# Attention over a long cache with a gated mix: projections in column blocks before the last sums, and the output written as four rows

## The chip, the cores and the metric

The kernel runs on one core of one Trainium2 chip. The metric is device time in microseconds (us). A run has a time and a span: the span, from the first to the last instruction on the core, is what the profile shows, and it lies about 1.8 us under the time. Every run told here was classed fast. Before the change the kernel takes 2521.2 us, so 0.1% is 2.5 us.

## The reference

One token `x` (512 numbers) attends to a cache of 65,536 keys and values for each of 32 heads; a small gated network takes the same token; a sigmoid gate mixes the two.

```
q = (x @ wq) as 32 heads of 128
p = softmax(q . k_cache / sqrt(128))            # 32 heads, 65536 keys each
a = (p . v_cache, the heads side by side) @ wo  # 4096 -> 512
b = (silu(x @ w_gate) * (x @ w_up)) @ w_down    # 512 -> 1792 -> 512
g = sigmoid(sum(x * gate_w))
return g * a + (1 - g) * b                      # 512 numbers in bf16, 1 KB
```

Keys and values are 1.07 GB and each is used once.

## The kernel before

Each head's cache comes in two chunks of 32,768 keys, so there are 64 chunks of keys and 64 of values. Three buffers of 8 MB take turns. For each chunk VectorE (DVE) multiplies the keys by the query ("products"), TensorE (PE) adds the 128 products of each key up to 8 partial sums with 16 matmuls against the identity ("sums"), DVE adds these 8 up ("gather"), ScalarE (ACT) takes exponentials, and PE multiplies by the values into `O_ps`. The loads of keys and values are issued by SyncE.

Only the end matters here. The last chunk (head 31, second half) is taken in four blocks of 64 keys a partition. Around it stand the projections of everything already known: `b_ps` (the gated network) and `a_ps` (heads 0 to 30).

```python
    def rows(key, w_v, names, cols, cname, ks):      # a projection to 512 outputs, 4 columns of 128
        group(key, [(m_x[:, b : b + 1],
                     [(w_v[:, k, bass.ds(b, P, OT)], cols[:, k : k + 1]) for k in ks])   # every 4th column
                    for b in range(OT)], names + [cname], ["m_x"])
    ...
    # last but one chunk, n == N - 2, after its fourth block:
                norm(0, H - 1)       # tot_ps: PE sums the row totals of heads 0..30; DVE inverts them
                outputs()            # oT = o_all * tot
    ...
    turn_outputs(1)
    rows("b_ps", wd, units(ws, 0, WO), hT, "hT", range(FT))              # 56 matmuls of one column
    diagonal()
    for i, j in enumerate(range(0, KPP, EK)):                            # four blocks
        block(n, j, EK)                                                  # products (DVE), sums (PE)
        if i == 0:
            dve("rest", ...)                                             # rest = (1 - g) * b
            rows("a_ps", wo, units(ws, WO, WL), M, "M", range(H))        # 128 matmuls of one column
        if i == 2:
            dve("rest2", ...)                                            # rest += g * a
        while len(todo) > 1:
            gather()
    gather()
    for m in V_END:                                                      # values in 5 pieces
        mms(("c", at), m_c[:, 0:1], [(v[:, j, :], P_sb[n % 2][:, j : j + 1]) ...])  # 256 one-column matmuls
        ...
    dve("o_last", ...)                                                   # m_c * tot
    rows("l_ps", wo_last, units(ws, WL, WL + D), o_last, "o_last", [0])  # 4 matmuls
    dve("out_sb", ...)                                                   # g * l + rest, 128 x 4
    dma("out", out[0, 0].rearrange("(p b) -> p b", b=OT), out_sb, ["out"], ["out_sb"])
```

The softmax here doesn't subtract the row's maximum and nothing guards it: scores larger than these inputs give would overflow.

## Time and profile before

| | before |
|---|---|
| time, median of the first 3 runs | 2521.22 us (2519.79 to 2521.41) |
| span of the profiled run | 2519.9 us |
| data queue's share of 16 DMA engines | 99.7% |
| PE busy, DVE busy | 79%, 50% |
| last values landed, last matmul into `m_c` done, end of span | 2511.9, 2514.7, 2519.9 us |

From the page, part 2 (busy tenths of the DMA engines in 40 slices) and part 3 (queue: packets, MB, share of 16 engines):

```profile
DMA  9999999999999999999999999999999999999998
q1 hardware_dynamic: 20880, 1087.78, 99.7%
```

The DMA engines are full from end to end. A change that moves no bytes can gain only in the last slice.

The timeline there: start, duration (both us), engine, source line, operation, output<-inputs, shapes, count, and in brackets the idle time before it and what ended it. `S_ps` are the sums; `m_x<-hT` is b_ps, `m_x<-M` is a_ps.

```profile
2466.23 15.46 PE L251 MATMUL O_ps<-slot_65,P_sb_83 128*4 128x512 bf16 x64 [1.35 <-ACT P_sb_83 L288]
...
2481.82 2.03 PE L279 MATMUL m_x<-hT,slot_66 128*128 128x1 bf16 x56
...
2484.98 3.40 PE L269 MATMUL S_ps_101<-slot_67,ident 128*128 128x512 bf16 x15
...
2488.22 4.38 PE L279 MATMUL m_x<-M,slot_66 128*128 128x1 bf16 x128
...
2492.68 5.08 PE L269 MATMUL S_ps_102<-slot_67,ident 128*128 128x512 bf16 x15
...
2498.41 4.42 DVE L338 TENSOR_TENSOR slot_67<-slot_67,q_bc_79 128x8192 bf16<-128x8192 bf16 x1
...
2506.35 3.35 PE L251 MATMUL m_c<-P_sb_84,slot_65 128*128 128x1 bf16 x128
...
2512.66 2.01 PE L251 MATMUL m_c<-P_sb_84,slot_65 128*128 128x1 bf16 x70 [1.22 <-issue]
2514.71 0.22 DVE L588 TENSOR_SCALAR o_last<-m_c,tot 128x1 bf16<-128x1 f32 x1 [4.38 <-PE m_c L251]
...
2515.38 0.22 DVE L593 SCALAR_TENSOR_TENSOR out_sb<-m_x,gval,rest 128x4 bf16<-128x4 f32 x1 [0.45 <-PE m_x L279]
2515.62 0.35 SPq L179 DMA_DIRECT2D out_dram<-out_sb  x1
```

The 256 matmuls into `m_c` take 8.3 us and contain a hole of 1.22 us ("issue": nothing that the profile shows was awaited). The semaphores in the trace say that the last values had landed at 2511.90, 0.76 us before the hole ended. From the issue of the output DMA to the end of the span it is 4.3 us, though the output is 1 KB.

From the view of a stretch of time, for 2482.89 to 2493.13 us (columns: us, busy time and count of PE, PE's weight loads, DVE, ACT, POOL, then the granted PE clock, 1.00 for whole and 0.50 for half, DMA share, GB/s); and from the DMA view (KB, and us from issue to landing):

```profile
2482.89:2493.13 10.24, 10.24 (x185) 6.36 (x165) 9.24 (x4) 0.35 (x2) 0.00 (x0) 1.00 1.04 445
```

```profile
out_dram<-out_sb SPq DMA_DIRECT2D x1, 1.0 KB, 3.0
```

### The profile page before, as it was taken

To read this page: it belongs to the slowest core of one execution; us is meant where nothing else is said; L and a number is where in the kernel's file an instruction comes from. 1 tells how busy PE (TensorE), PEld (TensorE's weight loads), DVE (VectorE), ACT (ScalarE), POOL (GpSimd) and SP (SyncE) were. 2 spreads that over 40 slices of the span, in tenths; PEclk is the share of its full clock that TensorE was granted. 3 is DMA by queue.
4 is the path that set the end of the run, shared out by engine and by line. 5 is a ranking of instruction groups with operands and counts; after the bars stand their busy time and mean duration, and the time that the engine had idled before them with its cause. 6 is when DMAs were issued, how large, how long until landed. Compare 5 with 4: busy or idle time off the path is not lost.

```text
span 2519.9 us, 15461 instructions
## 1 busy us (share of the span) xinstructions
PE 1980.9 (79%) x9115; PEld 410.4 (16%) x5153; DVE 1268.7 (50%) x290; ACT 97.9 (4%) x402; POOL 1.9 (0%) x9
## 2 busy tenths in 40 slices
PE   4787877877878778778787787787787877877888
PEld 1111111111111111111111111111111111111113
DVE  3455455464554554644645536446455455464454
ACT  0000000000000000000000000000000000000000
POOL 0000000000000000000000000000000000000000
PEclk8888988989889889899899899898988988989998
DMA  9999999999999999999999999999999999999998
GB/s 423 431 432 433 434 435 435 433 435 437 433 434 433 434 433 435 436 436 433 434 435 435 433 434 433 434 434 437 434 436 433 434 437 433 434 433 433 433 431 361
DMA packets 20903, 1088.04 MB, mean 432 GB/s; under 512 B 2450, under 2 KB 2580, under 8 KB 2836
## 3 DMA queue, kind: packets, MB, share of 16 engines
q1 hardware_dynamic: 20880, 1087.78, 99.7%
q8 instruction: 13, 0.21, 0.0%
q14 instruction: 6, 0.05, 0.0%
q10 hardware_dynamic: 4, 0.00, 0.0%
HBM read 1087.77 MB, written 0.00 MB: 432 GB/s over the span
## 4 chain that ended last, share of the span: by engine, by line
DMA 44%; PE 41%; DVE 13%; ACT 1%; issue 0%; another core or an unknown queue 0%; SPq 0%; DVEq 0%; ACTq 0%
PE O_ps L251 18%; DMA slot_67<-in_A_k_cache_dram 16%; DMA slot_65<-in_A_k_cache_dram 14%; DMA slot_66<-in_A_k_cache_dram 14%; PE S_ps_101 L269 11%; PE S_ps_102 L269 9%; DVE slot_67 L338 4%; DVE slot_66 L338 4%; DVE slot_65 L338 3%; DVE S_sb_82 L363 2%; PE m_c L251 1%; PE S_ps_101 L279 1%; PE m_x L279 1%; ACT P_sb_83 L288 1%; DMA slot_65<-in_A_wq_dram 0%; PE S_ps_102 L279 0%
## 5 line engine op out<-in xcount | busy, mean ns | idle before, releaser
L338 DVE TENSOR_TENSOR slot_67<-slot_67,q_bc_79 128x16384 bf16<-128x16384 bf16 (+1 forms) x28 | 208.2, 7469 | 143.8 <-DMA slot_67<-in_A_k_cache_dram 143.8
L363 DVE TENSOR_REDUCE S_sb_82<-S_ps_102 128x128 f32<-128x1024 f32 (+1 forms) x67 | 78.8, 1177 | 392.8 <-PE S_ps_102 L269 392.8
L338 DVE TENSOR_TENSOR slot_65<-slot_65,q_bc_78 128x16384 bf16<-128x16384 bf16 x22 | 190.2, 8689 | 146.9 <-DMA slot_65<-in_A_k_cache_dram 146.9
L338 DVE TENSOR_TENSOR slot_66<-slot_66,q_bc_78 128x16384 bf16<-128x16384 bf16 (+1 forms) x24 | 190.6, 7978 | 136.7 <-DMA slot_66<-in_A_k_cache_dram 121.2
L338 DVE TENSOR_TENSOR slot_66<-slot_66,q_bc_79 128x16384 bf16<-128x16384 bf16 x20 | 172.9, 8689 | 119.9 <-DMA slot_66<-in_A_k_cache_dram 119.9
L338 DVE TENSOR_TENSOR slot_65<-slot_65,q_bc_79 128x16384 bf16<-128x16384 bf16 x20 | 172.9, 8689 | 119.1 <-DMA slot_65<-in_A_k_cache_dram 119.1
L338 DVE TENSOR_TENSOR slot_67<-slot_67,q_bc_78 128x16384 bf16<-128x16384 bf16 x20 | 172.9, 8689 | 117.3 <-DMA slot_67<-in_A_k_cache_dram 117.3
L269 PE MATMUL S_ps_101<-slot_67,ident 128*128 128x512 bf16 x680 | 191.3, 450 | 0.0
L269 PE MATMUL S_ps_101<-slot_65,ident 128*128 128x512 bf16 x651 | 187.1, 458 | 0.0
L269 PE MATMUL S_ps_101<-slot_66,ident 128*128 128x512 bf16 x650 | 185.3, 455 | 0.0
L251 PE MATMUL O_ps<-slot_67,P_sb_83 128*4 128x512 bf16 x704 | 155.9, 383 | 27.9 <-ACT P_sb_83 L288 18.3
L251 PE MATMUL O_ps<-slot_65,P_sb_83 128*4 128x512 bf16 x704 | 155.2, 381 | 19.6 <-ACT P_sb_83 L288 19.6
L251 PE MATMUL O_ps<-slot_66,P_sb_84 128*4 128x512 bf16 x704 | 153.7, 379 | 19.3 <-ACT P_sb_84 L288 19.3
L251 PE MATMUL O_ps<-slot_65,P_sb_84 128*4 128x512 bf16 x640 | 139.7, 379 | 18.3 <-ACT P_sb_84 L288 18.3
L251 PE MATMUL O_ps<-slot_67,P_sb_84 128*4 128x512 bf16 x640 | 139.7, 379 | 18.3 <-ACT P_sb_84 L288 18.3
L251 PE MATMUL O_ps<-slot_66,P_sb_83 128*4 128x512 bf16 x640 | 139.7, 379 | 17.5 <-ACT P_sb_83 L288 17.5
L269 PE MATMUL S_ps_102<-slot_67,ident 128*128 128x512 bf16 x680 | 152.4, 382 | 0.0
L269 PE MATMUL S_ps_102<-slot_65,ident 128*128 128x512 bf16 x651 | 143.9, 379 | 0.0
L269 PE MATMUL S_ps_102<-slot_66,ident 128*128 128x512 bf16 x650 | 143.9, 379 | 0.0
L279 PE MATMUL S_ps_101<-slot_65,ident 128*128 128x512 bf16 x21 | 12.8, 608 | 134.5 <-DVE slot_65 L338 134.5
L279 PE MATMUL S_ps_101<-slot_66,ident 128*128 128x512 bf16 x22 | 13.1, 597 | 130.5 <-DVE slot_66 L338 130.5
L279 PE MATMUL S_ps_101<-slot_67,ident 128*128 128x512 bf16 x24 | 13.9, 580 | 125.4 <-DVE slot_67 L338 125.4
(89 smaller groups left out, 702.8 us busy)
## 6 DMA issues: line engine op xcount, KB each, us to landing
slot_66<-in_A_k_cache_dram SPq DMA_DIRECT2D x4, 2048.0 KB, 24.5
slot_67<-in_A_k_cache_dram SPq DMA_DIRECT2D x4, 2048.0 KB, 29.0
slot_65<-in_A_wq_dram SPq DMA_DIRECT2D x1, 4096.0 KB, 12.3
slot_66<-in_A_wo_dram SPq DMA_DIRECT2D x1, 4096.0 KB, 32.5
slot_65<-in_A_v_cache_dram SPq DMA_DIRECT2D x1, 4096.0 KB, 20.5
slot_65<-in_A_v_cache_dram SPq DMA_DIRECT2D x1, 2048.0 KB, 24.9
slot_65<-in_B_w_gate_dram SPq DMA_DIRECT2D x1, 1792.0 KB, 34.7
slot_65<-in_B_w_up_dram SPq DMA_DIRECT2D x1, 1792.0 KB, 38.4
```

The costliest lines, as they stand in the source:

```text
L251: ins = nc.tensor.matmul(out_ap, lhsT=a, rhs=b, start=start and i == 0, stop=stop and i == len(pairs) - 1,)
L269: ins = nc.tensor.add_instruction(mybir.InstMatmult(name=nc.get_next_instruction_name(), engine=mybir.EngineType.PE, ins=[nc.tensor.lower_ ...
L279: ins = nc.tensor.matmul(out_ap, lhsT=a, rhs=b, start=first, stop=last)
L288: "ACT", key, lambda: nc.scalar.activation(out=out_ap, in_=in_ap, func=func, **kw),
L338: "products", lambda: nc.vector.tensor_tensor(out=w, in0=w, in1=q_rep, op=ALU.mult),
L363: lambda: nc.vector.tensor_reduce(out=S_sb[b][:, :m], in_=S_ps[r][:, :m, :], axis=AXIS.X, op=ALU.add),
```

## The change

Intent: read the projection weights in contiguous blocks of 128 columns; do both projections before the last chunk's sums, so that they no longer stand between sums; take the row totals off the path of the last but one chunk; and write the output as 4 rows of 256 B instead of 128 pieces of 8 B. For the last, what is known of the output (`rest`, 128 x 4) is turned into 4 rows by one float32 matmul with an identity, and the last head's column is spread over `Z`, so that four matmuls give its part as 4 rows too.

```diff
-                    m_x[:, b : b + 1],
-                    [(w_v[:, k, bass.ds(b, P, OT)], cols[:, k : k + 1]) for k in ks],
+                    bank[:, b : b + 1],
+                    [(w_v[:, k, P * b : P * (b + 1)], cols[:, k : k + 1]) for k in ks],
 ...
+            if n == N - 2 and j == 2 * m:
+                sum_ps(0, H - 1)                       # PE's part of norm, two blocks earlier
             block(n, j, m)
 ...
-            elif n == N - 2 and j + m == KPP:
-                norm(0, H - 1)
-                outputs()
 ...                                                    # norm and outputs now after the last gather
-            turn_outputs(0)                            # now after O_ps
 ...
+    turn_outputs(0)
     turn_outputs(1)
-    rows("b_ps", ..., range(FT))
+    rows("b_ps", ..., range(FT), m_x, "m_x")
+    rows("a_ps", ..., range(H), m_sp, "m_sp")
     diagonal()
     for i, j in enumerate(range(0, KPP, EK)):
-        block(n, j, EK)
-        if i == 0:   (rest, a_ps)     if i == 2:   (rest2)
+        if i == 1:   (rest, rest2)
+        if i == 2:
+            mms("rest_ps", m_sp[:OT, :P], [(rest, ident_f)], ["rest", "ident_f"], ["m_sp"])
+            act("rest4", rest4, m_sp[:OT, :P], ACT.Copy, ["m_sp"], ["rest4"])
+        block(n, j, EK)
 ...
-    dve("o_last", ...)      rows("l_ps", ...)      out_sb 128 x 4
-    dma("out", out[0, 0].rearrange("(p b) -> p b", b=OT), ...)
+    dve("Z", lambda: nc.vector.tensor_scalar_mul(
+            Z[:, :: OT + 1], m_c[:, 0:1].to_broadcast([P, OT]), tot[:, h:H]), ...)
+    mms("l_ps", m_x[:OT, :P],
+        [(Z[:, OT * q : OT * (q + 1)], wo_last[:, 0, P * q : P * (q + 1)]) for q in range(OT)], ...)
+    dve("out_sb", ...)                                 # 4 x 128, with rest4
+    dma("out", out[0, 0].rearrange("(i p) -> i p", p=P), ...)
```

(Cut: tiles, memsets and selects at the start, wait lists.)

More of the change, by code (lines that the diff above doesn't have):

```diff
@@ L148 @@
     rest = sb("rest", [P, OT], f32)
+    rest4 = sb("rest4", [OT, P], f32)
+    ident_f = sb("ident_f", [P, P], f32)
+    Z = sb("Z", [P, OT * OT], bf16)
     o_row = sb("o_row", [H, Dh], bf16)
     M = sb("M", [P, H], bf16)
-    o_last = sb("o_last", [P, 1], bf16)
-    out_sb = sb("out_sb", [P, OT], bf16)
+    out_sb = sb("out_sb", [OT, P], bf16)
     S_ps = [psum.tile([P, HK, R], f32, name=f"S_ps{i}") for i in range(2)]
@@ L226 @@
     op("DVE", "oT0", lambda: nc.vector.memset(oT, 0.0), writes=["oT"])
+    op("DVE", "Z0", lambda: nc.vector.memset(Z, 0.0), writes=["Z"])
     op("DVE", "rowsum0", lambda: nc.vector.memset(rowsum, 0.0), writes=["rowsum"])
@@ L239 @@
     select("ident", ident, ones_b, "ones_b", [[-1, P]], 1)
+    select("ident_f", ident_f, ones, "ones", [[-1, P]], 1)
     select("pick", pick, ones[0:VB, 0:VB], "ones", [[-1, VB]], 1)
@@ L456, in gate, with rows @@
         )
-    def rows(key, w_v, names, cols, cname, ks):
+    def rows(key, w_v, names, cols, cname, ks, bank, bname):
         group(
@@ L468, in rows, with sum_ps @@
             ],
-            names + [cname], ["m_x"],
+            names + [cname], [bname],
         )
-    def norm(h0, h1):
+    def sum_ps(h0, h1):
         w = CH * RS
@@ L475, in norm @@
             ["ones", "rowsum"] + [("rowsum", i) for i in range(h0 * w, h1 * w)], ["m_x"])
+    def norm(h0, h1):
+        w = CH * RS
         dve(
@@ L539 @@
         if n == N - 2:
-            turn_outputs(0)
+            norm(0, H - 1)
+            outputs()
         pv(n)
@@ L553 @@
     load("v", n, V_END)
+    turn_outputs(0)
     turn_outputs(1)
-    rows("b_ps", wd, units(ws, 0, WO), hT, "hT", range(FT))
+    rows("b_ps", wd, units(ws, 0, WO), hT, "hT", range(FT), m_x, "m_x")
+    rows("a_ps", wo, units(ws, WO, WL), M, "M", range(H), m_sp, "m_sp")
     diagonal()
     for i, j in enumerate(range(0, KPP, EK)):
-        block(n, j, EK)
-        if i == 0:
+        if i == 1:
             dve("rest", lambda: nc.vector.tensor_scalar_mul(rest, m_x[:, :OT], ngval),
                 ["m_x", "ngval"], ["rest"])
-            rows("a_ps", wo, units(ws, WO, WL), M, "M", range(H))
-        if i == 2:
             dve(
@@ L566 @@
                 lambda: nc.vector.scalar_tensor_tensor(
-                    out=rest, in0=m_x[:, :OT], scalar=gval, in1=rest, op0=ALU.mult, op1=ALU.add
+                    out=rest, in0=m_sp[:, :OT], scalar=gval, in1=rest, op0=ALU.mult, op1=ALU.add
                 ),
-                ["m_x", "gval", "rest"], ["rest"],
+                ["m_sp", "gval", "rest"], ["rest"],
             )
+        if i == 2:
+            mms("rest_ps", m_sp[:OT, :P], [(rest, ident_f)], ["rest", "ident_f"], ["m_sp"])
+            act("rest4", rest4, m_sp[:OT, :P], ACT.Copy, ["m_sp"], ["rest4"])
+        block(n, j, EK)
         while len(todo) > 1:
@@ L585 @@
         if at == 0:
+            sum_ps(h, H)
             norm(h, H)
         at += m
-    dve("o_last", lambda: nc.vector.tensor_scalar_mul(o_last, m_c[:, 0:1], tot[:, h:H]),
-        ["m_c", ("tot", h)], ["o_last"])
-    rows("l_ps", wo_last, units(ws, WL, WL + D), o_last, "o_last", [0])
+    dve(
+        "Z",
+        lambda: nc.vector.tensor_scalar_mul(
+            Z[:, :: OT + 1], m_c[:, 0:1].to_broadcast([P, OT]), tot[:, h:H]
+        ),
+        ["m_c", ("tot", h)], ["Z"],
+    )
+    mms(
+        "l_ps", m_x[:OT, :P],
+        [(Z[:, OT * q : OT * (q + 1)], wo_last[:, 0, P * q : P * (q + 1)]) for q in range(OT)],
+        ["Z"] + units(ws, WL, WL + D), ["m_x"],
+    )
     dve(
@@ L593 @@
         lambda: nc.vector.scalar_tensor_tensor(
-            out=out_sb, in0=m_x[:, :OT], scalar=gval, in1=rest, op0=ALU.mult, op1=ALU.add
+            out=out_sb, in0=m_x[:OT, :P], scalar=gval[:OT, :], in1=rest4,
+            op0=ALU.mult, op1=ALU.add,
         ),
-        ["m_x", "gval", "rest"], ["out_sb"],
+        ["m_x", "gval", "rest4"], ["out_sb"],
     )
-    dma("out", out[0, 0].rearrange("(p b) -> p b", b=OT), out_sb, ["out"], ["out_sb"])
+    dma("out", out[0, 0].rearrange("(i p) -> i p", p=P), out_sb, ["out"], ["out_sb"])
     op("SP", "end", None, reads=["out"])
```

## The prediction

> **What bounds it.** The page gives the data queue 99.7% of sixteen DMA engines' span: 1,087.8 MB at 432 GB/s. The change leaves those bytes and the first 2,440 us alone; only the end can move. By the DMA view the last values land by about 2511.9 us; the span ends at 2519.9: at most 8 us (0.3%) are open.
>
> **The end before (timeline).** The last score sums end at 2506.4; 256 one-column matmuls into m_c run to 2514.68, at 26 ns each, with a hole of 1.22 us at 2511.44 put down to "issue". A 16 KB packet of the instruction queue starts at 2510.31 (DMA view), so I read the hole as instruction supply. [...] Then o_last 0.22, four matmuls 0.27, out_sb 0.22, the output DMA issued at 2515.62, 3.0 us to landing (DMA view), 1.3 us to the end.
>
> **What changes.**
> 1. Row totals of heads 0 to 30 are summed two blocks earlier. DVE's last two gathers of the last but one chunk no longer wait for them (2464.5 before; about 2459.4 and 2463.1 after), so its O_ps starts 2 us earlier (2466.2 before) and the last value loads are issued 2 us earlier. Worth nothing for landing: the queue is full of keys until 2492.
> 2. Projections use contiguous 128-column weights instead of every fourth column: 56 took 2.03 us and 128 took 4.38 (35 ns each), contiguous m_c ones 26 ns. Estimate: 1.5 and 3.4 us.
> 3. a_ps now stands before the last sums, and the second products wait for rest2, hence a_ps. Estimate: a_ps ends 2486.2 to 2487.3 (an instruction hole of up to 1 us may fall in it), second products start near 2487.4 instead of 2484.0. Before, a_ps sat between the sums and delayed the fourth products to 2498.4. Adding 4.42 + 0.69 us a block, these now begin 2497.0 to 2497.6, and m_c 0.3 to 1.6 us before 2506.35.
> 4. Turning rest into rows (a float32 matmul, about 0.4 us, and a copy, 0.25) hides behind products.
> 5. After m_c: Z costs what o_last did. Four 128-column matmuls at half clock: 0.3 to 0.6 us instead of 0.27; out_sb about 0.34 instead of 0.22. Together +0.3.
> 6. The output goes as 4 runs of 256 B instead of 128 of 8 B. [...] First and last completions lie 1.7 us apart before; I expect landing in 1.6 to 2.0 us, 1.0 to 1.4 less.
>
> The added memset and select at the start run while the first weights are awaited (13.4 us): free.
>
> **Sum.** m_c 0.7 earlier, tail +0.3, output DMA -1.2: -1.6 us, 0.06%. Predicted 2519.6 us, range 2516.5 to 2522.5. Chances: faster by over 2% 0.005, within 2% 0.99, slower 0.005.
>
> **What would show it.** Span about 2518.3; data queue still 99.7%; O_ps of the last but one chunk at 2464.2; a_ps at 26 ns each, before all of the last chunk's sums; fourth products near 2497.3; the m_c hole still there; output landing under 2.1 us.
>
> **What would make it wrong.** The clock halves for stretches of 3.4 us (about 2493.2 to 2496.6 before, windows view): elsewhere, it moves the sums by up to 1.7 us. A hole in a_ps may eat step 3's gain. Few descriptors may be slower than hoped. Runs before differ by 1.6 us, as much as the effect.

0.7 us earlier, 0.3 later and 1.2 less make -1.6 us, and 2519.6 us. The times of the work that is new (float32 matmul, copy, four 128-column matmuls, out_sb, landing) are estimates; after the change they measured 0.38, 0.27, 0.59, 0.34 and 1.17 us.

## The result, and the profile after

| | before | after |
|---|---|---|
| time, median of 4 runs | 2521.18 us | 2520.10 us (2518.92 to 2520.33) |
| span of the profiled run | 2519.9 | 2518.5 |
| start of b_ps | 2481.8 | 2479.2 |
| start of m_c | 2506.35 | 2507.52 |
| end of m_c | 2514.67 | 2514.75 |
| end of m_c to issue of the output DMA | 0.96 | 1.31 |
| issue of the output DMA to end of span | 4.26 | 2.47 |

The ratio of fast runs is 0.9996, with a 95% interval of 0.9979 to 1.0013. A ratio is the mean time of one kernel's fast runs over that of the other's of the same rounds, so not quite the ratio of the medians. That interval is some 4 us either way; what is argued below about single microseconds rests on the traces, and on runs side by side on one chip, where the scatter can be seen.

The same lines after the change. The page:

```profile
DMA  9999999999999999999999999999999999999998
q1 hardware_dynamic: 20744, 1087.78, 99.7%
```

The timeline (a_ps now writes `m_sp`):

```profile
2464.15 13.97 PE L255 MATMUL O_ps<-slot_65,P_sb_83 128*4 128x512 bf16 x64 [1.17 <-ACT P_sb_83 L292]
...
2479.23 1.55 PE L283 MATMUL m_x<-hT,slot_66 128*128 128x1 bf16 x56
...
2480.65 2.75 PE L283 MATMUL m_sp<-M,slot_66 128*128 128x1 bf16 x103
...
2485.19 0.82 PE L283 MATMUL m_sp<-M,slot_66 128*128 128x1 bf16 x25 [1.79 <-issue]
...
2486.19 4.42 DVE L342 TENSOR_TENSOR slot_67<-slot_67,q_bc_79 128x8192 bf16<-128x8192 bf16 x1
...
2488.14 5.87 PE L273 MATMUL S_ps_103<-slot_67,ident 128*128 128x512 bf16 x15
...
2494.05 0.69 DVE L367 TENSOR_REDUCE S_sb_81<-S_ps_103 128x64 f32<-128x512 f32 x1 [3.44 <-PE S_ps_103 L273]
...
2499.59 4.42 DVE L342 TENSOR_TENSOR slot_67<-slot_67,q_bc_79 128x8192 bf16<-128x8192 bf16 x1
...
2507.52 3.38 PE L255 MATMUL m_c<-P_sb_84,slot_65 128*128 128x1 bf16 x128
...
2511.20 3.55 PE L255 MATMUL m_c<-P_sb_84,slot_65 128*128 128x1 bf16 x128
...
2514.79 0.23 DVE L603 TENSOR_SCALAR Z<-m_c,tot 128x4 bf16<-128x4 f32 x1 [3.04 <-PE m_c L255]
...
2515.70 0.34 DVE L615 SCALAR_TENSOR_TENSOR out_sb<-m_x,gval,rest_97 4x128 bf16<-4x128 f32 x1 [0.68 <-PE m_x L255]
2516.06 0.34 SPq L181 DMA_DIRECT2D out_dram<-out_sb  x1
```

The stretch 2482.89 to 2493.13, and what SyncE waited for at the end (us in total, times, longest):

```profile
2482.89:2493.13 10.24, 8.45 (x66) 3.04 (x50) 4.55 (x2) 0.00 (x0) 0.00 (x0) 0.50 1.02 435
```

```profile
SPq L181 <- DMA out_dram<-out_sb: 0.8, 1, 0.8
```

What is to be seen: the last but one chunk's `O_ps` starts 2.1 us sooner and the projections are cheaper (27 ns instead of 35 for each matmul of a_ps). `O_ps` also takes 1.49 us less, which the change cannot be credited with: in the profile of before the clock was half for 3.41 us of it (2465.87 to 2469.28), and in none of the other 13, two of them of the old order. So of the 2.6 us by which b_ps starts sooner, 1.49 are the clock's; against them, the turning of the outputs now stands between `O_ps` and b_ps and takes 1.1 us. But a_ps has a hole of 1.79 us that was not there, the first sums run at half clock (5.87 us for 15 matmuls, where 3.40 is the full-clock figure), and the gather that waits for them comes at 2494.05. Nothing of the head start is left at the start of m_c; it comes 1.17 us later than before. The hole in m_c is gone instead, so m_c ends where it did. Then the tail is 0.36 us longer, and the output DMA lands 0.8 us after its issue is over, or 1.17 us after the issue began (by the trace's semaphores, 2516.06 to 2517.23), instead of 3.0. 0.08 + 0.36 - 1.79 us is the 1.4 us between the two spans.

### The profile page after: what moved, and what is told of

It reads as the page before. It is cut to its first block, busy times and chain, and to the rows that moved or that the text cites. A ratio compares the mean times of both kernels' runs of the same rounds, so it can differ in the third digit from the quotient of the medians.

```text
span 2518.5 us, 15470 instructions
## 1 busy us (share of the span) xinstructions
PE 1979.8 (79%) x9117; PEld 409.9 (16%) x5155; DVE 1268.7 (50%) x291; ACT 98.2 (4%) x403; POOL 2.2 (0%) x10
## 4 chain that ended last, share of the span: by engine, by line
DMA 44%; PE 41%; DVE 13%; ACT 1%; issue 0%; another core or an unknown queue 0%; SPq 0%; DVEq 0%; ACTq 0%
PE O_ps L255 18%; DMA slot_67<-in_A_k_cache_dram 16%; DMA slot_65<-in_A_k_cache_dram 14%; DMA slot_66<-in_A_k_cache_dram 14%; PE S_ps_103 L273 11%; PE S_ps_104 L273 9%; DVE slot_67 L342 4%; DVE slot_66 L342 4%; DVE slot_65 L342 3%; DVE S_sb_82 L367 2%; PE m_c L255 2%; PE S_ps_103 L283 1%; ACT P_sb_83 L292 1%; DMA slot_65<-in_A_wq_dram 0%; PE m_x L283 0%
```

## The experiments

Theory: the whole gain is the output DMA; the new order earns nothing, because with a_ps ahead of the sums PE meets a hole that is a wait for instructions and the clock halves, and because the end of m_c is pinned by other things (such a hole, the last values). Rivals: the order earns part of the gain; the holes are waits for data; the clock halves by its own rhythm; the second products' wait for rest2 sets the pace, as the prediction had it.

### The new output alone, and the new order alone

`e1_old_order` is the kernel before with the new output and contiguous weights, everything else in the old order; `e2_old_output` is the changed kernel with the old output.

```diff
  e1, on the kernel before:
+        if i == 3:  (rest_ps, rest4)     + Z, l_ps, out_sb 4 x 128, output as (i p) -> i p; contiguous rows()
  e2, on the changed kernel:
-    Z, l_ps, out_sb 4 x 128, rest_ps, rest4
+    o_last, l_ps, out_sb 128 x 4, output as (p b) -> p b; rows() with every 4th column
```

> The kernel before with the new output alone (four rows, Z, rows of rest turned by the float32 matmul, contiguous weights), the order of sums, totals and projections left as before. Theory A (the whole gain is the output DMA; the new order is worth nothing): output issue to end of the span about 2.5 us as in the changed kernel, against 4.3 before; m_c ends between 2513.0 and 2514.7; span 2517.0 to 2518.6. Theory B (the new order earned part of the gain): m_c ends at 2514.7 as before and the span is 2518.5 or more, and the old-output run with the new order shows a gain too.

> The changed kernel with the old output (128 rows of 4, strided weights, o_last), its order kept. Theory A (gain is the output DMA): output issue to end of span 4.3 us again, 1.8 us more than in the changed kernel; span 2519.5 to 2521, no better than before. Theory B: span under 2519.3.

Measured, both on one chip with before at 2522.0 us (median of 7):

| | time, median of 4 | span (profiled) | m_c start, end | output issue to end of span |
|---|---|---|---|---|
| e1: new output, old order | 2519.06 | 2518.4 | 2505.82, 2514.60 | 2.48 |
| e2: old output, new order | 2521.25 | 2519.6 | 2506.37, 2514.56 | 4.10 |

The gain goes with the output; the new order by itself is within the scatter (0.75 us under before, whose own runs differ by 2.6). Two things stay open here. The four rows need the contiguous weights, so e1 has both, and what the cheaper weight reads earn was not tested alone. And the tail explains 1.4 us; the medians of e1 and before differ by 2.9. e2 was expected at a span of 2519.5 to 2521, and its profiled run is there (the others: 2518.9 to 2519.6). In e1, m_c began 1.7 us sooner than in the changed kernel and still ended only 0.15 us sooner: there was a hole of 1.72 us in it.

### What the holes are

`e3_shift32` and `e4_shift95` add harmless one-column matmuls, each two instructions (the timeline of before lists 128 weight loads and 128 matmuls for a_ps), while PE is idle before the last but one chunk. They change no data and no waits near the end; they only move all later instructions in PE's program.

```diff
         m = EK if n in (0, N - 2) else HK
+        if n == N - 2:
+            mms("shift", m_x[:, 0:1], [(ones_b, ident[:, 0:1])] * 32, ...)     # e4: * 95
```

> The changed kernel with 32 one-column matmuls (64 instructions, weight load and matmul each) added in PE's idle time before the last but one chunk. Instruction supply: the hole in a_ps moves from after 103 matmuls to after 71 (a tolerance of 3), and a hole of 0.3 to 1.2 us may come back in the second part of m_c near its 25th matmul. Rival, a wait for data (weights wo, M) or the clock: the hole stays after 103 matmuls or at the same time, about 2483.4.

> The same with 95 one-column matmuls (190 instructions). Instruction supply: the hole in a_ps is gone, since its place is then about 8 matmuls into a_ps[...]; a_ps is 3.4 us in one piece and ends near 2484.1; a hole of about 1 us shows in the first part of m_c near its 92nd matmul. For the clock: if it drops near 2482.9 without any hole, the one-column matmuls and not the hole make it drop; if it does not drop, the hole did. Span within 1.5 us of the changed kernel.

The timeline of e3 (cut to a stretch):

```profile
2479.53 1.98 PE L283 MATMUL m_sp<-M,slot 128*128 128x1 bf16 x71
2484.03 1.68 PE L283 MATMUL m_sp<-M,slot 128*128 128x1 bf16 x57 [2.52 <-issue]
...
2511.94 2.91 PE L255 MATMUL m_c<-P_sb,slot 128*128 128x1 bf16 x104 [1.66 <-issue]
```

The hole moved from after 103 matmuls to after 71: by 32, exactly the number put in. A hole returned in m_c after 24 matmuls of its second part (25 expected; it took 1.66 us, where 0.3 to 1.2 were expected). Data cannot explain that; the weights wo had landed at 2472.8 in the changed kernel, and the place moved with the program, not with the time. So I read the holes as PE waiting for its own instructions. The queue that the profile names "instruction" has a packet before each: the page of the changed kernel counts 13 packets of q8, 0.21 MB, each of 16 KB in the trace (what such a packet brings is called a page in the recorded texts). One starts at 2482.77, where the DMA view shows, for 2482.7 to 2482.9 us:

```profile
q8 instruction: 1, 0.02, 27.5%
```

Matmuls resume 2.42 us later. Over all 20 holes in a_ps and m_c, in the profiles of the twelve experiments and of the two first kernels, from that packet to the resumption it took 2.19 to 2.45 us, wherever the hole was. From the end of a hole in a_ps, beside a full data queue (98.1% from 2480 to 2486 in the changed kernel), to the next packet it took 3.5 to 4.1 us (7 cases), from the end of one in m_c, with few values or none left to load, 1.1 to 1.6 us (13 cases). Whether the full queue makes this difference was not tested, and what sets a packet off the trace does not show. In the changed kernel's m_c the packet came at 2510.10, when the values were nearly all in; PE reached the place about 2512.8, 2.7 us after the packet, and there was no hole.

In e4 the hole in a_ps is gone, and a shorter one, which ends 2.24 us after the next packet, stands before the first sums:

```profile
2479.76 3.42 PE L283 MATMUL m_sp<-M,slot 128*128 128x1 bf16 x128
...
2485.38 0.61 PE L283 MATMUL S_ps<-slot,ident 128*128 128x512 bf16 x1 [0.41 <-issue]
```

The hole of m_c was not after 92 matmuls of the first part, as I expected, but after 89 of the second (1.33 us): there was a packet at 2488.96, long before PE reached the first place (15 us before m_c began). A miss in detail. e3 took 2519.85 us and e4 2518.90 (medians of 4, the chip of e1 and e2); in e4's profile the span is 2517.0 and m_c starts at 2504.17. The added matmuls leave the result correct.

### The clock

In e4 the granted clock was half from 2481.93 to 2488.75 though no hole had come before it, so here no hole made it fall. The stretch up to its 0.41 us hole, in the windows view (the clock is the third figure from the right):

```profile
2481.93:2484.97 3.04, 3.04 (x55) 2.93 (x52) 2.43 (x4) 0.00 (x0) 0.00 (x0) 0.50 1.00 420
```

`e8_wide` sets one 512-column matmul, its result thrown away, ahead of every 8 one-column matmuls of the projections.

```diff
+                if i % 8 == 0:
+                    nc.tensor.matmul(S_ps[1][:, :64, :], lhsT=ident, rhs=wo[:, 0, :], start=True, stop=True)
                 ins = nc.tensor.matmul(o, lhsT=a, rhs=c, start=first, stop=last)
```

> The changed kernel with one 512-column matmul (result thrown away) ahead of every 8 one-column matmuls of the two projections: 23 of them, about 5 us more of PE work before the first sums. If a stretch of one-column matmuls is what lets the clock halve: no half clock between 2478 and the end of the first sums, and the first sums take 3.8 us instead of 5.2 to 6.4. If the clock halves for another reason (its own rhythm, the DMA load, the wide matmuls before): half clock in 2480 to 2492 as in all five runs so far, and first sums of 5 us or more. Span within 2 us of the changed kernel.

Windows view of e8, for the projections and for the first sums (the granted clock is the third figure from the right):

```profile
2478.00:2488.60 10.60, 10.60 (x219) 7.81 (x215) 5.10 (x4) 0.20 (x1) 0.00 (x0) 1.00 1.02 433
2488.60:2492.40 3.80, 3.70 (x18) 0.15 (x2) 3.80 (x2) 0.00 (x0) 0.00 (x0) 1.00 1.09 466
```

The clock stayed whole and the first sums took 3.6 us, against 6.3 in the changed kernel. In the trace of before, the half-clock stretches that end before m_c last 3.41 us (8), 6.83 (46), 10.24 (10) and, once, 20.48. In the new order b_ps, a_ps and the one-column matmuls of the diagonal after them last 6.6 us (e4, no hole in them) to 9.7 us (e2); in all 9 profiles with that order and without the wide matmuls the clock halved 1.5 to 3.7 us after b_ps began, and the first sums met half clock. In all 14 profiles it also halved within 2.4 to 5.3 us of the start of m_c, the other long run of one-column matmuls. PE's busy time did not tell the two clocks apart: it was 3.04 of 3.04 us in e4's stretch at half clock and 10.60 of 10.60 in e8's at whole. In the old order sums met half clock in before and e1, and none did in `f_old_order` (below); why is not shown. The wide matmuls cost about 4.7 us themselves (from the start of b_ps to the end of a_ps 9.5 us, against 4.8 in e4), so e8 gains nothing: m_c began at 2505.81. Its time had two values, 2520.0 and 2523.8, twice each. The profile, the only one of e8, is of the faster kind. The slower kind stays unexplained; its mean granted clock is lower (0.904 and 0.905 against 0.907 and 0.908), so whether the clock stayed whole there too is not known.

### The wait for rest2

> The changed kernel with rest, rest2 and the turn to rows moved from the second block of the last chunk to the fourth, so that the second products no longer wait for a_ps. My prediction's step (the second products' wait for rest2 sets the pace): second products start near 2482.9 instead of 2486.2, the fourth products 2 to 3 us sooner, m_c starts near 2504.5 to 2505.5 and the span falls by 1 us or more. Rival (the first sums, which stand behind a_ps on PE and run at half clock, set the pace): second products start near 2482.9, but the first gather still waits for the first sums until 2492.4 to 2494.1, and m_c starts between 2505.9 and 2507.6, span 2518 to 2519, as in the changed kernel.

```diff
-        if i == 1:   (rest, rest2)     -        if i == 2:   (rest_ps, rest4)
+        if i == 3:   (rest, rest2, rest_ps, rest4)
```

Timeline of e5 (the second products, the first gather and what it waited for):

```profile
2483.08 4.42 DVE L342 TENSOR_TENSOR slot<-slot,q_bc 128x8192 bf16<-128x8192 bf16 x1 [0.97 <-DMA slot<-in_A_k_cache_dram]
...
2491.45 0.69 DVE L367 TENSOR_REDUCE S_sb<-S_ps 128x64 f32<-128x512 f32 x1 [3.94 <-PE S_ps L273]
```

The second products started 3.1 us sooner and the time was not used: DVE then waited 3.94 us for the first sums, which came sooner (2491.45) than the rival's 2492.4 to 2494.1. m_c started at 2505.31, 2.2 us sooner than in the changed kernel, which lies in the range that the prediction's step would have given; but b_ps itself began 2.2 us sooner in this run (2477.03). From b_ps to m_c it was 28.3 us in both (some 0.4 us of e5's are the moved operations, which now stand before its fourth products). The scatter in b_ps's start (2476.8 to 2479.2 in the profiles of the new order) goes with the clock in the chunk before: no half-clock stretch there between 2440 and 2450 us, 2476.8 to 2477.2; one of 3.4 us, 2478.0 to 2478.3; one of 6.8 us, as in the changed kernel's first profile, 2479.2. So from here on I compare b_ps to m_c. The rival stands: the first sums, behind a_ps on PE, set the pace. The time was 2519.69 us.

### The output DMA

`e7_16x64` and `e7_64x16` send other data of the same 1 KB in other shapes. Their outputs are wrong, which doesn't matter for the times.

```diff
+    out_w = sb("out_w", [16, 32], bf16)        # or [64, 8]
+    dve("out_w", ...)                          # fills it, after out_sb: the issue comes 0.26 us later
-    dma("out", out[0, 0].rearrange("(i p) -> i p", p=P), out_sb, ["out"], ["out_sb"])
+    dma("out", out[0, 0].rearrange("(i p) -> i p", p=32), out_w, ["out"], ["out_w"])
```

> The changed kernel with the output DMA sending 16 rows of 64 B of other data instead of 4 of 256 B; wrong result on purpose, to read the time from issue to the last completion (1.2 us for 4 of 256 B, 2.8 to 3.0 us for 128 of 8 B). If the many completions of 16 engines are slow: 2.4 us or more. If the tiny pieces[...] are slow: 1.1 to 1.6 us.

> The same with 64 rows of 16 B, wrong on purpose. If the pieces' size or number sets it: between the 16 x 64 B and the 128 x 8 B case, 1.6 to 2.4 us. If only the 16 completions do: the same as 16 x 64 B.

DMA views of the two, 16 rows of 64 B and then 64 rows of 16 B (last figure: us from issue to landing):

```profile
out_dram<-out_w SPq DMA_DIRECT2D x1, 1.0 KB, 1.3
```

```profile
out_dram<-out_w SPq DMA_DIRECT2D x1, 1.0 KB, 1.7
```

So 4 x 256 B, 16 x 64 B, 64 x 16 B and 128 x 8 B land in 1.17, 1.3, 1.7 and 2.8 to 3.0 us. Sixteen completions are not slow: those of 16 x 64 B and of 64 x 16 B come within 0.17 us of one another, those of 128 x 8 B (before) within 1.72 us. Size or number does it, with the largest step between 16 and 8 B. Why 8 B is so much worse stays open; I could not part the size from the number, as the output is 1 KB. Both kernels took 2520.2 us (medians of 2).

### Side by side, five rounds

Four kernels on one chip: the changed one again (`f_after`), e1 again (`f_old_order`), e4 again (`f_shift95`), and `e6_a_between`, the changed kernel with a_ps put back between the sums, and `rest` and its turn behind it.

```diff
  e6, on the changed kernel:
-    rows("a_ps", ...)                          # before the loop over blocks
         block(n, j, EK)
+        if i == 0:
+            rows("a_ps", ...)
     (rest, rest2, rest_ps, rest4 at i == 3)
```

> The changed kernel once more, beside the others of this call on one chip. Span 2517 to 2519; hole in a_ps after 103 matmuls; in m_c a hole after 56 or 57 matmuls unless the m_c matmuls start after about 2507.3 (the page comes about 2.35 us after its fetch shows in the DMA view). A second profile also tells how much of the last chunk's start is its own scatter (O_ps end 2475.5 to 2478.2 so far).

> The kernel before with the new output alone, again. If the new order is worth nothing: within 0.7 us of the changed kernel, either way.

> The changed kernel with 95 one-column matmuls ahead, again: no hole in a_ps; m_c starts near 2504 and ends near 2513.2, with the last values landed by 2512.0 to 2512.6. Faster than the changed kernel by 0.7 to 1.8 us and faster than before by 2 to 3.5 us if instruction supply is what held the changed kernel; no difference from the changed kernel if the first result was scatter.

> The changed kernel with a_ps put back after the first sums of the last chunk and rest2 and the turn to rows after it (row totals early, contiguous weights and four-row output kept). If placing a_ps ahead cost time: from the start of b_ps to the start of m_c 27.2 us or less instead of 28.0 to 28.4. Either way the end of m_c is set by the instruction page and the last values (2513 to 2514.5), so the span is within 0.8 us of the changed kernel.

| 5 runs each | time, median (range) | b_ps to m_c, us | m_c start, end | ratio to before |
|---|---|---|---|---|
| before (9 runs) | 2521.05 (2520.37 to 2521.87) | 24.5 (first profile) | 2506.35, 2514.67 (first profile) | 1 |
| f_after | 2518.76 (2518.56 to 2520.06) | 27.4 | 2504.20, 2513.02 | 0.9993 |
| f_old_order | 2518.46 (2518.11 to 2518.79) | 23.1 | 2502.34, 2512.84 | 0.9989 |
| f_shift95 | 2519.01 (2518.14 to 2519.18) | 27.3 | 2505.29, 2513.57 | 0.9990 |
| e6_a_between | 2519.71 (2518.40 to 2520.11) | 27.4 | 2505.49, 2514.22 | 0.9992 |

No fast run of the four with the new output was as slow as the fastest of before. (Even f_old_order's interval, 0.9976 to 1.0003, holds 1.) By medians they gain 1.3 to 2.6 us, of which the tail explains 1.4; as before was not profiled in this round, what lies beyond is not assigned. Among the four, the ranges overlap, and the order of kernels is not settled. f_after had its holes where they were expected, after 103 matmuls of a_ps and 56 of the second part of m_c; its span, 2516.8, was 0.2 us under the expected range. f_shift95 was expected 0.7 to 1.8 us under f_after and was not (medians 0.25 us above): a miss. Its a_ps had no hole, but its half-clock stretch was 10.24 us long this time (6.8 in e4), and m_c started 1.1 us later than in e4; f_after for its part had no half-clock stretch in the chunk before and started m_c 3.3 us sooner than the changed kernel's first profile. e6 was expected at 27.2 us or less from b_ps to m_c and had 27.4, with half clock on its first sums, and its median was 0.95 us over f_after's, not within 0.8: a miss as well. The distance is not a fair measure for e6, though: the first products cannot start before their keys land (2477.6 to 2478.0 in all profiles), and without a_ps in front PE waited 1.84 us for them, after b_ps and the diagonal.

f_old_order shows why little more is to be had from the order. Its profile has no half clock between 2446.7 and 2504.8, and m_c started 5.2 us sooner than in the changed kernel's first profile; then it waited for the values. Its timeline:

```profile
2509.81 1.01 PE L256 MATMUL m_c<-P_sb,slot 128*128 128x1 bf16 x32 [0.49 <-DMA slot<-in_A_v_cache_dram]
2511.03 0.59 PE L256 MATMUL m_c<-P_sb,slot 128*128 128x1 bf16 x16 [0.21 <-DMA slot<-in_A_v_cache_dram]
2512.26 0.58 PE L256 MATMUL m_c<-P_sb,slot 128*128 128x1 bf16 x16 [0.64 <-DMA slot<-in_A_v_cache_dram]
2512.88 0.23 DVE L598 TENSOR_SCALAR Z<-m_c,tot 128x4 bf16<-128x4 f32 x1 [6.30 <-PE m_c L256]
```

The last values landed at 2512.21, as in every kernel within half a microsecond (2511.9 to 2512.5), and m_c ended 0.6 us later. An earlier m_c cannot end sooner with these loads, as its last piece of values comes then; the changed kernel's first profile is 1.9 us above this end of m_c, its second 0.2.

The version to keep is thus the old order with the new output: the lowest median of the four, fewer edits, and the tightest range. It is 2.6 us (0.1%) under before, by medians; over the changed kernel its 0.3 us is not settled.

## Why the prediction was right or wrong

The total was right: 2519.6 us predicted, 2520.1 measured, and "within 2%" with near certainty. Luck had a part in it: by the traces m_c gave 0.8 us less than said and the output DMA 0.6 us more, and these errors nearly cancel. The stated range, 2516.5 to 2522.5, held the time of before as well, so a change without any effect would have fitted it. Three terms made the total up.

1. "output DMA -1.2" was right in kind and too small: it measured -1.79, 1.17 us to landing where I gave 1.6 to 2.0. I took what is left with few pieces as larger than it is.
2. "tail +0.3" measured +0.36: Z 0.23, four matmuls 0.59, out_sb 0.34, as costed.
3. "m_c 0.7 earlier" is the step that failed. By its end m_c was 0.08 us later, by its start 1.17 later. Inside it:
   - Row totals earlier: right. `O_ps` was said to start at 2464.2 and started at 2464.15; landing times did not move.
   - Contiguous weights at 26 ns: right (27 ns in the first 103 matmuls of a_ps).
   - "second products wait for rest2, hence a_ps": true and without consequence. e5 took the wait away and the distance from b_ps to m_c stayed 28.3 us. The sum "adding 4.42 + 0.69 us a block" followed DVE, where PE's first sums were the later of the two: the second products started at 2486.19, sooner than said, but the first sums ended at 2494.0, DVE waited 3.44 us for them, and so the fourth products started at 2499.59, not 2497.0 to 2497.6.
   - The hole in a_ps was foreseen ("up to 1 us") and was 1.79.
   - The clock was named as a risk "by up to 1.7 us" at a stretch of 3.4 us elsewhere. I read it as a rhythm that may fall anywhere. In these profiles it goes with the work: the change joined the one-column matmuls to one stretch of 8.6 us, and the clock was half for 10.24 us from 3.7 us into it. In e8's one profile, with wide matmuls among them, it stayed whole.
   - "the m_c hole still there": wrong in the profile of the result (no hole), right in f_after (1.78 us). Whether it shows went with the start of m_c: in the 13 other profiles m_c started 1.15 us or more sooner, and a hole stood in it.

The gain expected of the order was not lost to one thing. It was first taken by PE (hole and clock), and where a run escaped these, a hole in m_c or the last values took it. "Off the critical path" would be too simple: m_c's end is a race of three things that arrive within 2 us.

## What to carry to other kernels

Where the DMA engines are full to the end, look first at what follows the last landing, and count the output's pieces there: 128 pieces of 8 B took 1.8 us longer than 4 of 256 B. One-column matmuls in long runs cost more here than their 26 ns: in them PE stood idle up to 2.52 us at one place, with a packet of the instruction queue 2.19 to 2.45 us before the next matmul, and the clock fell to half in them, so that the wide matmuls after them ran slower (15 in 5.87 us instead of 3.40). Before crediting a reordering with a microsecond, repeat the profile: here the start of b_ps moved by 2.4 us between two profiles of one kernel.
